# Linear attention into two expert layers: batches 2 and 3 of k and v loaded in the first visits, x written over its squares, eight weight preparations ahead of the units, stores one step behind

## The chip, the cores and the metric

The kernel runs on one core of a Trainium2 chip. The metric is the device time of one execution in microseconds (us). A core has TensorE (PE, matrix products), VectorE (DVE), ScalarE (ACT), GpSimd (POOL) and SyncE (SP); here SP issues every DMA, in program order. Each engine runs its own instructions in order and waits on semaphores of the others. TensorE's clock has two levels, 1.2 and 2.4 GHz; a granted clock of 1.00 is the upper one.

## The reference

```
kv  = einsum('bhsd,bhse->bhde', k, v)            # 4 batches, 8 heads, 576 tokens, 64 wide
out = einsum('bhsd,bhde->bhse', q, kv)
out = out / sqrt(mean(out*out, -1) + 1e-6) * g_norm
x   = out as [2304 tokens, 512]
h   = x @ w_in                                   # 512 -> 2048
x   = (h * sigmoid(h)) @ w_out                   # 2048 -> 512
out = ((x @ w_a) * (x @ w_b)) @ w_out2           # 512 -> 1536 -> 512
```

q, k, v and g_norm are float32. The weight matrices come as float64 values; the kernel reads them as pairs of 32-bit words, rebuilds a float32 number from them, and splits that into a high and a low part, so that a product of two float32 matrices is three passes of TensorE (high by high, low by high, high by low).

## The kernel before, in words

The 2304 tokens are six blocks of 384 (a block is called j). Work goes in steps. A step belongs to one slice of 128 of the 2048 hidden columns and one block: `h_mm` (12 matmuls into `hp`), the gate `g` on ACT (L409), its high part `gh` on ACT (L355) and low part `gl` on DVE (L360), and 12 matmuls `x1p` (L371) that add the slice of the step before to the four output columns. `VISITS` lists which block takes which slices, and a running number g counts the steps: g = 4 to 31 are the first visits (blocks 0, 1 and 2), where the raw weights `raw_wi` and `raw_wo` also arrive and are decoded on DVE (shift L302, low word L308, sign L315, low part L330); g = 32 to 63 are the visits of blocks 2 and 3, where the weights are already there. After that come eight units u, each a seven-product (Winograd) scheme for two slices and the blocks 4 and 5 together (`seven`, `unit`; matmuls X_h, Y_h, V_h, Z_h; DVE additions L660, L663, L792). Then phase 3 computes products with w_a, w_b and w_out2 by the same scheme.

What else has to happen is hung on the steps by number: `at(g, f)` runs f after the x1p of step g, and `early[g]` runs it between `gh` and `gl` of step g, so that DVE does it ahead of the `gl` for which the next x1p waits. `at_unit(h, f)` hangs f on hook h of the units, four hooks to a unit. Hung there are:

- attention: `load_kv` and `load_kvt` (L114, L122) bring k and v, `kv_pair` multiplies them (`kvps`, L180) and copies the result to `kvc`; `load_q_blocks`, `turn_q` (DVE transpose `qT`, L153), `attend` (matmuls `ao` L214, squares `sq` on ACT L220, sum `ss` on DVE L225, the power -0.5 `rr` on POOL L230), `norm_mul` (`xn`, DVE L235) and the transposes `xtp` (PE L248). Before, k and v of batches 2 and 3 are loaded at g = 33 to 51 and multiplied two steps later;
- `sums(u)` (L728 to L739): sums of the decoded w_in slices that the units need, stored to DRAM (`hsd`) and read back;
- `prepare(wa or wb, pair)`: loads, decodes and combines two slices of w_a or w_b and stores the result (`wd`) for phase 3. There are twelve. Before, six start at g = 36, 42, 48, 54, 58 and 62 and six in the units;
- `combine(0, kt)`: the sums of blocks 0 and 1 of the second layer's input (`hB`, `hT`, `T`), stored to `xcd`.

Buffers are pools that rotate: `page` 37 tiles of 4 KB, `mid` 6 tiles (qT, xn, T and hT and others, in order of allocation), and two tiles of squares that carry the 1e-6 in an extra column. A new tile waits for the last reader of the one whose place it takes. SP issues DMAs in order, so a DMA that waits for a buffer holds up all behind it.

Of the kernel before, what the change touches and what calls it, by code (L numbers as in the profile page):

```python
# [59 lines left out]
def tile_linattn_moe_moe2(ctx: ExitStack, tc: tile.TileContext, q, k, v, g_norm,  # L60
# [21 lines left out]
    sq = [sb.tile([P, CH, 2, D + 1], F32, tag=f"sq{i}", name=f"sq{i}") for i in range(2)]  # L82
# [13 lines left out]
    def mid(shape, dt, name):  # L96
        return sb.tile(shape, dt, tag="mid", bufs=6, name=name)

    def six(shape, dt, name):
# [6 lines left out]
           for b in range(2) for p in range(NP)}  # L106
    kvc.update({(b, p): kvc[b % 2, p] for b in range(2, B) for p in range(NP)})
# [110 lines left out]
    def norm_square(j, p):  # L218
        sq.reverse()
        nc.scalar.activation(sq[0][:, :, :, 0:D], ao[j, p], AF.Square, scale=D ** -0.5)  # L220
        xn[j, p] = sq[0]

    def norm_mean(j, p):
        ss = sb.tile([P, CH, 2], F32, tag="ss", bufs=3, name=f"ss_{j}_{p}")
        nc.vector.reduce_sum(ss, xn.pop((j, p)), axis=AX.X)  # L225
        rms[j, p] = ss
# [6 lines left out]
    def norm_mul(j, p):  # L233
        xn[j, p] = mid([P, CH, 2, D], F32, f"xn_{j}_{p}")
# [196 lines left out]

    def combine(d, kt, place, blocks=None, keep=None, home=None):
# [47 lines left out]
    def prepare(kind, p):  # L480
# [24 lines left out]
        def rest():  # L505
            for f in wait.pop(0):
                f()
# [171 lines left out]
    PLACES = {"mid": 6, "sig": 2, "gh": 2, "gl": 2}  # L679
    ab = {}  # L680

    def products(d, p, after=None, more=(), more_b=()):

        a = {}
        for n, got in enumerate(seven_ab(d, p, 0, "mid")):
            if n == 2 and after is not None:
                after()
            if got is not None:
                f, i, z, u = got
                t = a[f, i] = sb.tile([P, TB], F32, tag="mid", bufs=6, name=f"a_{d}_{p}_{f}{i}")  # L690
# [29 lines left out]
    def sums(u):  # L720
# [5 lines left out]
        def add():  # L726
            for t, (hi, lo) in zip(s, (w0, w1_)):
                nc.vector.tensor_add(t[:, 0].bitcast(F32), hi.bitcast(F32), lo.bitcast(F32))  # L728
            a11, a12, a21, a22 = (t[:, 0, h * H2:(h + 1) * H2].bitcast(F32) for t in s for h in range(2))
# [6 lines left out]
        def split():  # L736
            for t in s:
                nc.scalar.copy(t[:, 0], t[:, 1].bitcast(F32))
                nc.vector.tensor_sub(t[:, 1], t[:, 1].bitcast(F32), t[:, 0].bitcast(F32))  # L739
# [7 lines left out]
        return add, split, store  # L747
# [142 lines left out]
    at(base[5] - 2, load_kvt, 2)  # L890
    at(base[5] + 6, load_kvt, 3)
    for i, (p, j) in enumerate([(p, 3) for p in range(NP)] + [(p, j) for p in (0, 2, 1, 3) for j in (4, 5)]):
        g0 = base[5] + 1 + 2 * i
        if j != 5:
            b = 2 if j == 3 else 3
            at(g0 - 2, load_kv, b, p)
            at(g0, kv_pair, b, p)
# [10 lines left out]

    for n in range(2 * NPAIR):
        load, steps = prepare(("wa", "wb")[n % 2], n // 2)  # L910
        if n < 6:
            g0 = base[5] + (4, 10, 16, 22, 26, 30)[n]
# [9 lines left out]
        else:  # L922
            h0 = 1 + 5 * (n - 6)
            if n == 6:
                at(base[6] + 15, load)
            else:
                at_unit(h0 - 3, load)
# [330 lines left out]
```

## Time and profile before

| | us |
|---|---|
| median of 3 runs | 881.21 (881.09 to 881.83) |
| profiled execution | 884.84 |
| its span, first to last instruction | 883.0 |
| PE busy | 861.4 (98%) |
| DVE busy | 604.3 (68%) |
| ACT busy | 330.7 (37%) |
| POOL busy | 51.9 (6%) |

The profiled execution is 3.6 us above the median of the runs. Its mean granted TensorE clock is 0.995. A row of the chain of waits has its start, its duration and what ran; a row of a timeline has start, duration, engine, line, operation, tiles and, in brackets, how long the engine sat idle before it and what it waited for. A row of the view by stretches has the stretch, then busy time and count of each engine in it, the granted clock, the share of the DMA engines and GB/s. A row of waits has who waited for whom, us in total, times, and the longest. A busy PE is a modelled figure: a matmul's end is put some way past the start of the next one.

### The profile page before, as it was taken

To read this page: it belongs to the slowest core of one execution; us is meant where nothing else is said; L and a number is where in the kernel's file an instruction comes from. 1 tells how busy PE (TensorE), PEld (TensorE's weight loads), DVE (VectorE), ACT (ScalarE), POOL (GpSimd) and SP (SyncE) were. 2 spreads that over 40 slices of the span, in tenths; PEclk is the share of its full clock that TensorE was granted. 3 is DMA by queue.
4 is the path that set the end of the run, shared out by engine and by line. 5 is a ranking of instruction groups with operands and counts; after the bars stand their busy time and mean duration, and the time that the engine had idled before them with its cause. 6 is when DMAs were issued, how large, how long until landed. Compare 5 with 4: busy or idle time off the path is not lost.

```text
span 883.0 us, 13575 instructions
## 1 busy us (share of the span) xinstructions
PE 861.4 (98%) x5015; PEld 818.0 (93%) x5015; DVE 604.3 (68%) x1153; ACT 330.7 (37%) x670; POOL 51.9 (6%) x53
## 2 busy tenths in 40 slices
PE   7999999999899999999999999999999999999998
PEld 4799999999899999999999999999999999999996
DVE  3879997848356778787626788886556665545555
ACT  4666654426334555545323523321232211121110
POOL 4420001001111100000000000000000000000000
PEclk9999999999899999999999999999999999999999
DMA  9942890866675378999499789496787476765001
GB/s 268 354 178 98 227 331 15 287 209 193 195 235 178 107 265 313 377 372 355 185 422 419 309 335 339 172 368 263 252 292 266 155 248 265 283 217 191 1 1 71
DMA packets 123650, 212.19 MB, mean 240 GB/s; under 512 B 41024, under 2 KB 85568, under 8 KB 123584
## 3 DMA queue, kind: packets, MB, share of 16 engines
q1 hardware_dynamic: 123584, 211.33, 67.8%
q8 instruction: 39, 0.64, 0.3%
q14 instruction: 27, 0.22, 0.1%
HBM read 143.92 MB, written 67.37 MB: 239 GB/s over the span
## 4 chain that ended last, share of the span: by engine, by line
PE 84%; DVE 7%; DMA 4%; SPq 2%; issue 2%; ACT 1%; POOL 0%; DVEq 0%; POOLq 0%; ACTq 0%
PE x1p L371 19%; PE op L830 17%; PE hp L345 12%; PE Z_a L653 4%; PE V_b L653 4%; PE X_b L653 4%; PE Z_b L653 4%; PE X_a L653 4%; PE V_a L653 4%; PE Y_b L653 2%; PE Y_a L653 2%; PE Z_h L653 2%; DMA kvt<-in_v_dram 2%; PE V_h L653 2%; PE X_h L653 1%
## 5 line engine op out<-in xcount | busy, mean ns | idle before, releaser
L371 PE MATMUL x1p<-gh,wo 128*128 128x384 f32 x768 | 193.9, 335 | 0.0
L371 PEld LDWEIGHTS x1p<-gh,wo 128*128 128x128 f32 x768 | 138.9, 188 | 0.0
L371 PE MATMUL x1p<-gl,wo 128*128 128x384 f32 x384 | 127.9, 337 | 1.4 <-DVE gl L360 1.4
L345 PE MATMUL hp<-xh,wi 128*128 128x384 f32 x512 | 104.8, 345 | 0.4 <-ACT xh L252 0.3
L360 DVE TENSOR_TENSOR gl<-g,gh 128x384 fp32r<-128x384 f32 x96 | 54.2, 565 | 59.0 <-ACT gh L355 58.6
L345 PEld LDWEIGHTS hp<-xh,wi 128*128 128x128 f32 x512 | 89.3, 190 | 1.8 <-ACT xh L252 1.0
L830 PE MATMUL op<-wp,ab 128*128 128x512 f32 x360 | 83.4, 390 | 0.0
L712 ACT CAST ab<-a 128x384 fp32r<-128x384 f32 x72 | 37.0, 514 | 115.3 <-DVE a L706 58.2
L830 PEld LDWEIGHTS op<-wp,ab 128*128 128x128 f32 x360 | 67.4, 188 | 13.7
L371 PEld LDWEIGHTS x1p<-gl,wo 128*128 128x128 f32 x384 | 72.0, 188 | 2.5 <-DVE gl L360 2.3
L838 DVE TENSOR_TENSOR o<-op,o 128x512 f32<-128x512 f32 x90 | 60.4, 685 | 16.4 <-PE op L830 16.3
L830 PE MATMUL op<-w,ab 128*128 128x512 f32 x288 | 66.9, 390 | 0.0
L830 PEld LDWEIGHTS op<-w,ab 128*128 128x128 f32 x288 | 53.9, 188 | 10.9
L355 ACT CAST gh<-g 128x384 fp32r<-128x384 f32 x96 | 49.3, 514 | 28.4 <-PE x1p L371 26.2
L345 PE MATMUL hp<-xl,wi 128*128 128x384 f32 x256 | 55.7, 338 | 0.0
L409 ACT ACTIVATE g<-hp 128x384 f32<-128x384 f32 x64 | 31.3, 490 | 63.8 <-PE hp L345 63.7
L230 POOL TENSOR_TENSOR rr<-ss,nhalf 128x6 f32<-128x6 f32 x24 | 35.7, 1491 | 228.0 <-DVE ss L225 227.9
L345 PEld LDWEIGHTS hp<-xl,wi 128*128 128x128 f32 x256 | 45.9, 190 | 0.4 <-DVE xl L256 0.3
L653 PE MATMUL X_a<-xc,wp 128*128 128x384 f32 x216 | 43.7, 337 | 0.7 <-ACT u_a L658 0.7
L653 PE MATMUL Z_a<-xc,wp 128*128 128x384 f32 x216 | 43.4, 335 | 0.1
L653 PE MATMUL Z_b<-xc,wp 128*128 128x384 f32 x216 | 43.4, 335 | 0.1
L653 PE MATMUL V_b<-xc,wp 128*128 128x384 f32 x216 | 43.3, 335 | 0.0
(177 smaller groups left out, 1424.1 us busy)
## 6 DMA issues: line engine op xcount, KB each, us to landing
wp<-wd SPq DMA_DIRECT2D x114, 512.0 KB, 6.4
xc<-xcd SPq DMA_DIRECT2D x21, 768.0 KB, 8.5
hw<-hsd SPq DMA_DIRECT2D x24, 512.0 KB, 7.3
raw_wi<-in_moe_w_in_dram SPq DMA_DIRECT2D x16, 512.0 KB, 7.5
raw_wo<-in_moe_w_out_dram SPq DMA_DIRECT2D x16, 512.0 KB, 7.5
hsd<-hs SPq DMA_DIRECT2D x16, 512.0 KB, 4.2
raw_wa<-in_moe_w_a_dram SPq DMA_DIRECT2D x12, 512.0 KB, 6.6
wd<-s_wa SPq DMA_DIRECT2D x12, 512.0 KB, 3.6
```

The costliest lines, as they stand in the source:

```text
L230: nc.gpsimd.tensor_tensor(r, rms[j, p], nhalf, op=ALU.pow)
L345: nc.tensor.matmul(o, w[wp][:, kt * P:(kt + 1) * P], x[key][:, kt, :], start=(n == 0), stop=(n == 3 * KD - 1))
L355: nc.scalar.copy(gh, src)
L360: nc.vector.tensor_sub(gl, src, gh.bitcast(F32))
L371: nc.tensor.matmul(acc[vi][c], w[wp][:, c * P:(c + 1) * P], gg[vi, s][g], start=(s == s0 and i == 0), stop=(s == s1 - 1 and i == 2))
L409: nc.scalar.activation(g, o, AF.Silu)
L653: nc.tensor.matmul(b[bank], w(name, wq, kt), x(i, xq, kt), start=(fresh and k == 0), stop=(k == 5), skip_group_check=True)
L712: nc.scalar.copy(o[:, 0], t)
L830: nc.tensor.matmul(o, ab[d, p, f, n][:, g, ts], wp[p, 7 + f][:, wq * DM:(wq + 1) * DM], start=(k == 0), stop=(k == 5))
L838: nc.vector.tensor_add(t, o, t)
```

## The change

k and v of batches 2 and 3 are loaded and multiplied at g = 11 to 26. Batch 3's products get tiles of their own (`kvc`), batch 2 still takes those of batch 0. For blocks 3 to 5 `xn` is written over the tile that held its squares, and POOL writes the 1e-6 column again before each of these squares; `mid` goes from 6 tiles to 5. Eight preparations of w_a and w_b start at g = 34, 38, ... 62 and four in the units, at other hooks. The stores of `prepare` go through a list that `flush` empties one step later. The parts of `sums` are spread over more hooks and begin at other steps. `combine(0)` is hung before the preparations, so that it comes first where both share a step.

```diff
@@ -79,7 +79,9 @@
-    sq = [sb.tile([P, CH, 2, D + 1], F32, tag=f"sq{i}", name=f"sq{i}") for i in range(2)]
+    sqs = [sb.tile([P, TB + 2 * CH], F32, tag=f"sq{i}", name=f"sq{i}") for i in range(2)]
+    sq = [(t.rearrange("p (c r d) -> p c r d", c=CH, r=2),
+           t[:, 0:TB].rearrange("p (c r d) -> p c r d", c=CH, r=2)) for t in sqs]
     x1d = dr.tile([NB - 2, P, KD, TB], F32, tag="x1d", name="x1d")
@@ -94,7 +96,7 @@
     def mid(shape, dt, name):
-        return sb.tile(shape, dt, tag="mid", bufs=6, name=name)
+        return sb.tile(shape, dt, tag="mid", bufs=5, name=name)
@@ -103,8 +105,8 @@
     kvc = {(b, p): sb.tile([P, P], F32, tag=f"kvc{b}_{p}", name=f"kvc_{b}_{p}")
-           for b in range(2) for p in range(NP)}
-    kvc.update({(b, p): kvc[b % 2, p] for b in range(2, B) for p in range(NP)})
+           for b in (0, 1, 3) for p in range(NP)}
+    kvc.update({(2, p): kvc[0, p] for p in range(NP)})
     qs, qT, xn, ao, rms, xt = {}, {}, {}, {}, {}, {}
@@ -217,12 +219,14 @@
         sq.reverse()
-        nc.scalar.activation(sq[0][:, :, :, 0:D], ao[j, p], AF.Square, scale=D ** -0.5)
+        if j >= 3:
+            nc.gpsimd.memset(sq[0][0][:, :, :, D:], 1e-6)
+        nc.scalar.activation(sq[0][0][:, :, :, 0:D], ao[j, p], AF.Square, scale=D ** -0.5)
         xn[j, p] = sq[0]
...
         ss = sb.tile([P, CH, 2], F32, tag="ss", bufs=3, name=f"ss_{j}_{p}")
-        nc.vector.reduce_sum(ss, xn.pop((j, p)), axis=AX.X)
+        nc.vector.reduce_sum(ss, xn[j, p][0], axis=AX.X)
         rms[j, p] = ss
@@ -231,7 +235,7 @@
     def norm_mul(j, p):
-        xn[j, p] = mid([P, CH, 2, D], F32, f"xn_{j}_{p}")
+        xn[j, p] = xn[j, p][1] if j >= 3 else mid([P, CH, 2, D], F32, f"xn_{j}_{p}")
         nc.vector.tensor_mul(xn[j, p], ao.pop((j, p)), rms.pop((j, p)).unsqueeze(3).broadcast_to([P, CH, 2, D]))
@@ -429,6 +433,14 @@
+    fresh_, due = [], []
+
+    def flush():
+        while due:
+            due.pop(0)()
+        due.extend(fresh_)
+        fresh_.clear()
+
@@ -503,8 +515,9 @@
         def rest():
-            for f in wait.pop(0):
-                f()
+            sub, *put_ = wait.pop(0)
+            sub()
+            fresh_.extend(put_)
@@ -676,7 +689,7 @@
-    PLACES = {"mid": 6, "sig": 2, "gh": 2, "gl": 2}
+    PLACES = {"mid": 5, "sig": 2, "gh": 2, "gl": 2}
     ab = {}
@@ -687,7 +700,7 @@
                 f, i, z, u = got
-                t = a[f, i] = sb.tile([P, TB], F32, tag="mid", bufs=6, name=f"a_{d}_{p}_{f}{i}")
+                t = a[f, i] = sb.tile([P, TB], F32, tag="mid", bufs=5, name=f"a_{d}_{p}_{f}{i}")
                 if u is None:
@@ -723,9 +736,11 @@
-        def add():
+        def whole():
             for t, (hi, lo) in zip(s, (w0, w1_)):
...
+
+        def add():
             a11, a12, a21, a22 = (t[:, 0, h * H2:(h + 1) * H2].bitcast(F32) for t in s for h in range(2))
@@ -733,9 +748,12 @@
-        def split():
+        def high():
             for t in s:
...
+
+        def low():
+            for t in s:
                 nc.vector.tensor_sub(t[:, 1], t[:, 1].bitcast(F32), t[:, 0].bitcast(F32))
@@ -744,7 +762,7 @@
-        return add, split, store
+        return whole, add, high, low, store
@@ -887,14 +905,13 @@
-    at(base[5] - 2, load_kvt, 2)
-    at(base[5] + 6, load_kvt, 3)
+    for b, g0 in ((2, 11), (3, 18)):
+        at(g0, load_kvt, b)
+        for p in range(NP):
+            at(g0 + 2 * p - p // 3, load_kv, b, p)
+            at(g0 + 3 + 2 * p - p // 3, kv_pair, b, p)
     for i, (p, j) in enumerate([(p, 3) for p in range(NP)] + [(p, j) for p in (0, 2, 1, 3) for j in (4, 5)]):
         g0 = base[5] + 1 + 2 * i
-        if j != 5:
-            b = 2 if j == 3 else 3
-            at(g0 - 2, load_kv, b, p)
-            at(g0, kv_pair, b, p)
         at(g0 - 5, load_q_blocks, j, p)
@@ -906,10 +923,17 @@
+    todo = [f for kt in range(2) for f in combine(0, kt, mid)]
+    for n, fs in enumerate(todo):
+        for f in fs:
+            if n % 2:
+                at(base[5] + 1 + n // 2, f)
+            else:
+                early.setdefault(base[5] + 1 + n // 2, []).append(f)
     for n in range(2 * NPAIR):
         load, steps = prepare(("wa", "wb")[n % 2], n // 2)
-        if n < 6:
-            g0 = base[5] + (4, 10, 16, 22, 26, 30)[n]
+        if n < 8:
+            g0 = base[5] + 2 + 4 * n
             at(g0 - 3, load)
@@ -920,20 +944,13 @@
         else:
-            h0 = 1 + 5 * (n - 6)
-            if n == 6:
+            h0 = 3 + 7 * (n - 8)
+            if n == 8:
                 at(base[6] + 15, load)
             else:
-                at_unit(h0 - 3, load)
+                at_unit(h0 - 4, load)
             for i, f in enumerate(steps):
                 at_unit(h0 + i, f)
-    todo = [f for kt in range(2) for f in combine(0, kt, mid)]
-    for n, fs in enumerate(todo):
-        for f in fs:
-            if n % 2:
-                at(base[5] + 1 + n // 2, f)
-            else:
-                early.setdefault(base[5] + 1 + n // 2, []).append(f)
     made = []
@@ -942,10 +959,12 @@
     for u in range(NF1 // 2):
-        g0 = (8, 12, 15, 18, 25, 26, 28, 29)[u]
+        g0 = (7, 10, 14, 17, 23, 25, 27, 29)[u]
         at(g0, begin_sums, u)
-        at(g0 + 1, lambda u: made[u][1](), u)
-        at(g0 + 2, lambda u: made[u][2](), u)
+        early.setdefault(g0 + 1, []).append(lambda u=u: made[u][1]())
+        at(g0 + 1, lambda u: made[u][2](), u)
+        early.setdefault(g0 + 2, []).append(lambda u=u: made[u][3]())
+        at(g0 + 3, lambda u: made[u][4](), u)
     homes = []
@@ -1057,9 +1076,9 @@
     nc.gpsimd.memset(nhalf, -0.5)
-    for t in sq:
+    for t, _ in sq:
         nc.gpsimd.memset(t[:, :, :, D:], 1e-6)
-    for t in [kvc[b, p] for b in range(2) for p in range(NP)]:
+    for t in [kvc[b, p] for b in (0, 1, 3) for p in range(NP)]:
         nc.gpsimd.memset(t, 0.0)
@@ -1158,8 +1177,8 @@
                     then += [d1.begin, d1.step]
-                between = [d1.begin] if j < 2 else early.get(g, [])
-                step1(vi, s, prev, side.get(-g, []) + then + side.get(g, []), between)
+                between = ([d1.begin] if j < 2 else []) + early.get(g, [])
+                step1(vi, s, prev, [flush] + side.get(-g, []) + then + side.get(g, []), between)
                 prev = (vi, s)
@@ -1171,10 +1190,10 @@
             left = []
-            for h, k in enumerate((0, 2, 3, 6)):
+            for h, k in enumerate((0, 2, 4, 6)):
                 hooks[k] += inner.get(4 * u + h, [])
-            hooks[3] += both(g)
-            hooks[6] += both(g + 1)
+            hooks[3] += [flush] + both(g)
+            hooks[6] += [flush] + both(g + 1)
             for n, to, i in (((0, 1, 0), (0, 1, 2)) if u == 0 else ()) + (
@@ -1182,7 +1201,7 @@
             g += 2
-        for f in left:
+        for f in left + [flush, flush]:
             f()
...
             gg[8, s] = split_pair(g1[s // 4][:, s % 4], f"5_{s}")
```

Three places show how the order of the work moves. The first is SP's queue. Before, the loads of batch 3's first pair (`kv_3_0`, k and v of heads 0 and 1) stand behind stores of `combine` and `prepare` (`xcd`, `wd`), in step 39, two steps ahead of the product that needs them:

```order
L122 DMA kvt_3_2448<-in_k_dram 64x8x64
L122 DMA kvt_3_2448<-in_v_dram 64x8x64
L145 DMA qb_5_0_2467<-in_q_dram 32x12x32 x4
L430 DMA wd_72<-s_0_wa0_2425 128x1024
L430 DMA wd_72<-s_1_wa0_2426 128x1024
L430 DMA wd_72<-m_wa1_2333 128x512
L114 DMA kv_3_0_2533<-in_k_dram 128x2x256
L114 DMA kv_3_0_2533<-in_v_dram 128x2x256
L282 DMA raw_wb0_2536<-in_moe2_w_b_dram 128x4x256
```

After, SP issues them in step 18, between the raw loads of the slices 13 to 15 (`raw_wi`, `raw_wo`) and the stores of `sums`:

```order
L286 DMA raw_wo13_1428<-in_moe_w_out_dram 128x1024
L147 DMA qb_2_3_1456<-in_q_dram 32x12x32 x4
L124 DMA kvt_3_1474<-in_k_dram 64x8x64
L124 DMA kvt_3_1474<-in_v_dram 64x8x64
L116 DMA kv_3_0_1478<-in_k_dram 128x2x256
L116 DMA kv_3_0_1478<-in_v_dram 128x2x256
L286 DMA raw_wi14_1500<-in_moe_w_in_dram 128x4x256
L286 DMA raw_wo14_1558<-in_moe_w_out_dram 128x1024
L116 DMA kv_3_1_1595<-in_k_dram 128x2x256
L116 DMA kv_3_1_1595<-in_v_dram 128x2x256
L760 DMA hsd_69<-wi_6_866 128x1024
L761 DMA hcd_70<-wi_7_960 128x2x256
```

In the queue the k load of `kv_3_0` goes from row 133 to row 83 counted from the start; the raw loads of slices 14 and 15 now stand behind loads that were not there.

The second place is ACT's queue near step 44, where `combine(0, 1)` makes its last piece, `hT4_0_1`. Before:

```order
L409 ACTIVATE g_5_11_2737<-hp_5_11_2724 128x384
L355 CAST gh_5_11_2739<-g_5_11_2737 128x384
L428 CAST hB21_0_1_2744<-x1_0_704 128x384
L428 CAST a_wb0_2770<-m_wb0_2718 128x512
L428 CAST hT4_0_1_2775<-T4_0_1_2722 128x384
L409 ACTIVATE g_5_12_2793<-hp_5_12_2780 128x384
L355 CAST gh_5_12_2795<-g_5_12_2793 128x384
L888 ACTIVATE xf_4_2822<-xtp_4_0_2825,g2_64 128x384
L220 ACTIVATE sq0_66<-ao_5_0_2830 128x6x64
```

After:

```order
L413 ACTIVATE g_5_11_2827<-hp_5_11_2814 128x384
L359 CAST gh_5_11_2829<-g_5_11_2827 128x384
L432 CAST hB21_0_1_2831<-x1_0_712 128x384
L432 CAST hT4_0_1_2856<-T4_0_1_2808 128x384
L432 CAST a_wa1_2861<-m_wa2_2810 128x512
L413 ACTIVATE g_5_12_2883<-hp_5_12_2870 128x384
L359 CAST gh_5_12_2885<-g_5_12_2883 128x384
L906 ACTIVATE xf_4_2911<-xtp_4_0_2914,g2_64 128x384
L224 ACTIVATE sq0_66<-ao_5_0_2919 128x6x64
```

The rows read alike, but with five `mid` tiles instead of six `hT4_0_1` takes the place of `qT_5_0`, so this cast now waits for the matmuls `ao_5_0` on PE, and the gate of slice 12 stands behind it.

The third place is DVE's queue at the first unit. Before, from the additions `u2_h_0` and `u3_h_0` to the first `gl` of the units:

```order
L660 TENSOR_TENSOR u2_h_0_3835<-Y_h_0_3849,u2_h_0_3835 128x384
L663 TENSOR_TENSOR u3_h_0_3864<-V_h_0_3857,u2_h_0_3835 128x384
L403 COPY x1_3_3866<-x1p_6_1_3088 128x384
L403 COPY x1_3_3866<-x1p_6_3_3090 128x384
L429 TENSOR_TENSOR s_0_wb2_3839<-s_0_wb2_3839 128x512
L429 TENSOR_TENSOR s_1_wb2_3840<-s_1_wb2_3840 128x512
L429 TENSOR_TENSOR m_wb5_3774<-m_wb5_3774 128x256
L302 TENSOR_SCALAR m_wa6_3887<-m_wa6_3887 128x512
L308 SCALAR_TENSOR_TENSOR m_wa6_3887<-raw_wa6_3823,m_wa6_3887 128x512
L315 SCALAR_TENSOR_TENSOR m_wa6_3887<-raw_wa6_3823,m_wa6_3887 128x512
L792 TENSOR_TENSOR h_0_11_3919<-Z_h_0_3912,u3_h_0_3864 128x384
L360 TENSOR_TENSOR gl_4_0_3921<-g_4_0_3897,gh_4_0_3899 128x384
```

After:

```order
L673 TENSOR_TENSOR u2_h_0_3909<-Y_h_0_3922,u2_h_0_3909 128x384
L676 TENSOR_TENSOR u3_h_0_3937<-V_h_0_3930,u2_h_0_3909 128x384
L407 COPY x1_3_3939<-x1p_6_1_3181 128x384
L407 COPY x1_3_3939<-x1p_6_3_3183 128x384
L810 TENSOR_TENSOR h_0_11_3979<-Z_h_0_3972,u3_h_0_3937 128x384
L364 TENSOR_TENSOR gl_4_0_3981<-g_4_0_3966,gh_4_0_3968 128x384
L433 TENSOR_TENSOR s_0_wb3_3912<-s_0_wb3_3912 128x512
L433 TENSOR_TENSOR s_1_wb3_3913<-s_1_wb3_3913 128x512
L433 TENSOR_TENSOR m_wb7_3848<-m_wb7_3848 128x256
L810 TENSOR_TENSOR h_0_10_3996<-V_h_0_3930,u2_h_0_3909 128x384
```

Three splits (L429) and three decode operations of `m_wa6` no longer stand ahead of `h_0_11`; the splits of the preparation before come behind `gl`, and `m_wa6` is decoded earlier.

## Rows read from the trace of the kernel before

**Rows 1.** busy time by stretch, core 0: the first visits, one dip, the units
```profile
67.00:130.00 63.00, 62.64 (x363) 62.33 (x362) 59.05 (x116) 38.96 (x75) 1.84 (x1) 1.00 0.73 218
...
200.00:240.00 40.00, 36.31 (x245) 34.32 (x244) 23.93 (x49) 17.02 (x39) 5.41 (x4) 0.91 0.62 195
...
340.00:430.00 90.00, 87.52 (x501) 86.75 (x501) 70.79 (x143) 47.56 (x95) 0.00 (x0) 1.00 0.88 330
```

**Rows 2.** waits of PE over the whole span
```profile
PE kvps L180 <- DMA kv<-in_v_dram: 4.8, 3, 2.6
...
PE ao L214 <- DVE qT L153: 2.6, 3, 1.1
...
PE Z_h L653 <- DVE h L792: 1.4, 1, 1.4
...
PE V_h L653 <- DVE h L792: 1.0, 1, 1.0
...
PE x1p L371 <- DVE gl L360: 1.4, 3, 0.8
```

**Rows 3.** chain of waits from 205 to 250 us
```profile
220.95 5.60 DMA kv<-in_v_dram
...
226.64 1.33 PE kvps L180 x20
...
227.98 4.14 PE hp L345 x12
...
232.12 2.52 PE x1p L371 x12
...
236.98 2.11 PE hp L345 x12
```

**Rows 4.** timeline of PE, one kv pair on the upper clock
```profile
181.65 0.69 PE L180 MATMUL kvps<-kv 128*64 128x64 f32 x16
182.17 0.29 PE L180 MATMUL kvps<-kvt 128*64 128x64 f32 x4
```

**Rows 5.** timeline of PE, the wait at 131 us
```profile
132.30 0.91 PE L214 MATMUL ao<-kvc,qT 128*128 128x128 f32 x6 [1.08 <-DVE qT L153]
```

**Rows 6.** timeline of DVE, 125 to 130 us
```profile
125.53 0.68 DVE L330 TENSOR_TENSOR wi<-m_wi,wi 128x512 fp32r<-128x512 f32 x1
...
126.13 0.68 DVE L315 SCALAR_TENSOR_TENSOR m_wo<-raw_wo,m_wo 128x512 uint32<-128x512 uint32 x1
...
127.53 0.55 DVE L360 TENSOR_TENSOR gl<-g,gh 128x384 fp32r<-128x384 f32 x1
...
129.30 0.56 DVE L235 TENSOR_TENSOR xn<-ao,rr 128x384 f32<-128x384 f32 x1 [1.22 <-POOL rr L230]
```

**Rows 7.** timeline of POOL, two powers
```profile
127.43 1.84 POOL L230 TENSOR_TENSOR rr<-ss,nhalf 128x6 f32<-128x6 f32 x1 [77.65 <-DVE ss L225]
...
143.56 1.32 POOL L230 TENSOR_TENSOR rr<-ss,nhalf 128x6 f32<-128x6 f32 x1 [6.84 <-DVE ss L225]
```

**Rows 8.** timeline of DVE at 197 us
```profile
197.10 0.58 DVE L153 STREAM_TRANSPOSE qT<-qb 128x384 f32<-128x384 f32 x1 [4.22 <-PE xtp L248]
```

**Rows 9.** waits of SP from 44 to 450 us
```profile
SPq L745 <- DVE hs L739: 74.3, 5, 34.1
```

**Rows 10.** DMA issues of raw_wo: KB each, us from issue to landing
```profile
raw_wo<-in_moe_w_out_dram SPq DMA_DIRECT2D x16, 512.0 KB, 7.5
```

**Rows 11.** tile kv, its loads
```profile
DMA to landing us min/median/max: 2.6/4.3/8.8
```

**Rows 12.** groups of DVE, 67 to 200 us, a 256-wide sum
```profile
L731 DVE TENSOR_TENSOR hs<-hs 128x256 f32<-128x256 f32 x8 | 3.4, 426 | 0.3
```

**Rows 13.** costliest groups of the page, the high part on ACT
```profile
L355 ACT CAST gh<-g 128x384 fp32r<-128x384 f32 x96 | 49.3, 514 | 28.4 <-PE x1p L371 26.2
```

**Rows 14.** waits of ACT from 60 to 340 us
```profile
ACT hT L428 <- PE ao L214: 14.9, 2, 8.8
```

**Rows 15.** timeline of POOL at the start
```profile
1.45 1.08 POOL L1063 MEMSET kvc<- 128x128 f32 x7
```

## The prediction

> **What bounds the kernel now.** I read the busy shares by stretch first. PE is the bound: 87.5 of 90 us in the units, 62.64 of 63 us in the first visits [rows 1]. So only time in which PE waits, or runs on the lower clock, can be won. The one stretch with a lower clock is 200 to 240 us, at 0.91, with PE busy for 36.3 of 40 us [rows 1]. The waits of PE then name who ended them: the loads of k and v 4.8 us in three waits, the longest 2.6; the turned q 2.6 us in three; `gl` 1.4 us in three; DVE's additions `h` in the units 1.4 and 1.0 us [rows 2]. Last I followed the chain through 205 to 250 us for the worst one: a v load that took 5.60 us to land, then `kvps`, then 12 matmuls of `hp` in 4.14 us and 12 of `x1p` in 2.52, where a later row has 2.11 for the same 12 of `hp` [rows 3]. A wait row understates its loss by about 0.17 us, since a 128x384 matmul is shown with 0.34 us and the next starts 0.17 us after it; I add that to each.
>
> **What can be won at most.** Five places. (a) At 226 us: 2.64 + 0.17 for the wait. Behind it the clock is at the lower level: `hp` takes 4.14 - 2.11 = 2.03 too long, `x1p` 2.52 - 2.11 = 0.41, and the pair itself 1.33 against 182.17 + 0.29 - 181.65 = 0.81 for one at the upper level, so 0.52 [rows 3, 4]. Together 5.8. (b) The three waits for `qT`: 2.6 + 0.5 = 3.1 [rows 2], of which the one at 131 us is 1.08 + 0.17 = 1.25 [rows 5]. (c) The three for `gl`: 1.4 + 0.5 = 1.9. (d) The two for `h`: 2.4 + 0.3 = 2.7. Sum 13.5. The other two kv waits are at the start, which the change does not touch.
>
> **The change part by part.**
>
> *k and v in the first visits.* The wait of (a) goes, with its clock: at g = 33 to 53 no load is waited for any more, because `kv_3_0` is multiplied in step 21. Worth 5.8. Each of the eight pairs still costs PE its 0.81 us, now between g = 14 and 26; that is moved and not added. What is late next is the raw weights. kv loads land in 2.6 to 8.8 us [rows 11], raw loads in 7.5 [rows 10], and SP issues in order: `raw_wo14` takes the page of a k or v tile that PE reads in step 19 and cannot be issued earlier, about 121 us on the clock of before. It then lands at 121 + 7.5 = 128.5, and its decode stands on DVE and ACT for about 129.7. So some 1 us is left, and `raw_wi14`, two steps before, has about none. Bounds: nothing, or a wait as long as the present one with the clock lost, 5.8. I take nothing, since DMA is busy 0.73 there [rows 1] and the stores of `sums`, on which SP stood 74.3 us waiting for DVE in five waits, one of 34.1 [rows 9], now enter SP's queue a step later, when their data is done.
>
> The Trainium skill's "DMA: Bandwidth & Descriptors", section "Anatomy of one DMA", gives a fit of about 2.0 us plus bytes over 436 GB/s, for loads issued by GpSimd; for these 512 KB an estimate from it is 3.2 us. The trace has 7.5, more than twice that, and I go by the trace; by the fit the raw loads would have 4 us to spare, the first and second rival below would have no ground, and the sum would not change.
>
> *POOL.* Four more `kvc` memsets at the start: seven take 1.08 us [rows 15], so some 0.6 us, ahead of the memset of `kvt` that the first products read. If nothing hid it, that is +0.6; PE waits there for k and v loads anyway [rows 2], so I take 0. The twelve memsets of the squares' extra column are smaller still and run on an engine with 5.4 us of work in 40 [rows 1]: 0 to 0.15 us each if one ended a wait; 0. Each waits for the transposes of the `xn` two attends back, done by then; behind it on POOL stands only the power of its own attend, and ACT's square waits for it.
>
> *Batch 2's `kvc` and DVE at g = 20 to 22.* At 131 us `qT` came late because DVE stood 1.22 us for the power `rr` [rows 6]. In the changed order a kv pair's 0.81 us lies on PE ahead of this `ao`, so DVE is given that much. Between 0 and 1.25 remain; I take 1.25 - 0.81 = 0.4 left, 0.85 won.
>
> This power took 1.84 us; one that ran with DVE idle took 1.32 [rows 7]. Beside the first DVE ran `gl`, a subtraction of two SBUF tiles [rows 6]. The Trainium skill's "SBUF — State Buffer", section "Who interferes with whom", says that a DVE instruction with two SBUF inputs and a GpSimd one that reads SBUF block each other; the trace agrees, with 0.52 us. It speaks against this change, because `sums` and `prepare` are made of such instructions and now stand beside more of the powers: by it the 0.85 would be 0.3.
>
> *`xn` over its squares, `mid` from 6 to 5.* Before, `qT` took the place of an older `xn`, so it waited 4.22 us for PE's transposes and then came late [rows 8]; there are two such places, at 197 and 235 us, each 0.76 + 0.17 = 0.93. After, no `xn` of these blocks is in `mid`, and the places are freed by stores or casts. Both go: 1.9. The new wait is `hT4_0_1` on ACT in step 44, for `ao_5_0` on PE. Behind it on ACT stand a cast of `a_wa1`, the gate of slice 12 and its `gh`; on DVE two subtractions, four 256-wide sums of 0.43 [rows 12], and the `gl`. From the end of `ao_5_0` that is two ACT casts of 0.51 [rows 13] or so, then on DVE 0.60 for a 512-wide operation (they start 0.60 apart [rows 6]), four of 0.35 to 0.43 and 0.56: about 3.8 us. PE has one `hp` of 2.11 and two matmuls, 2.45, before it needs that `gl`. So PE waits 1.4. From below the cost is nothing, if the kernel's ACT waits for `ao` of before, 14.9 us in two [rows 14], are a measure: they ended no wait of PE. I take 1.4, because here the gate stands right behind. It comes where before a `gl` wait of 0.75 + 0.17 was.
>
> *Sums and preparations on other steps.* At g = 8 to 11 the rows of DVE between two `gl`, counted from the order at 0.60 for 512-wide, 0.47 for 384-wide and 0.35 for 256-wide, come to 5.6, 4.0, 5.2 and 5.6: 20.4 us against four steps of 4.2, so 3.6 too much. `gl` can lead by one `hp` and two matmuls, 2.45. PE waits about 1.2, where before 0.36 + 0.17 stood in step 10. At 211 us the prepare rows ahead of `gl` move to other steps, and 0.46 goes. In (c) then: 0.53 + 0.46 + 0.92 = 1.9 before, 1.2 + 1.4 = 2.6 after, so 0.7 lost. Ahead of the units DVE gets 14.3 us more over g = 34 to 63: two preparations, less the sums that move up. In 200 to 240 it is busy 23.9 of 40 [rows 1], and the heaviest step there has 6.2 against 4.2 with light ones beside it, so it holds.
>
> *Units.* Four preparations instead of six. Ahead of `h_0_11` three splits (0.60 + 0.60 + 0.35) and three decode operations (0.35 + 0.60 + 0.60), 3.1 us, go, against a wait of 1.4; at 367 us four sums and a split leave in the same way. I take 2.5 of the 2.7.
>
> **The sum.** 5.8 + 0.85 + 1.9 - 0.7 + 2.5 = 10.3. From the profiled execution, 884.84 - 10.3 = 874.5; it stands 3.6 above the median of 881.21, so the runs should have 870.9. Phase 3 is left as it is: PE is full there, and of `mid` its tiles wait a product longer back.
>
> **Rivals.** 1. Half of it is given back in 75 to 140 us. DVE is busy 59 of 63 us there [rows 1], the raw loads have 0 to 1 us of room, and `sums` come a step earlier. Two waits of the size of the present kv one, 2.8 each without a lost clock: 10.3 - 5.6 = 4.7, time 876.5. Against it: DVE's total in the stretch is the same.
> 2. Slower. The same raw loads, but late by more than a few us: SP stands at `raw_wo14` for its page and everything behind it is late too, `raw_wi15` and `raw_wo15` among it. From the point where PE waits as long as 2.6 us the clock is lost as in [rows 3], and each costs 5.8. Three of them, 17.4, against 10.3 won: 888.3. Against it: such pages were waited for before, and PE lost no clock there (1.00 in 67 to 130 [rows 1]).
> 3. No change: what PE gets back is waited for at the next `gl`, because DVE with 14.3 us more is the bound from g = 32 on. Then (a) to (d) turn into `gl` waits, 880.5. Against it: DVE busy about 24 + 69 of 140 us there and 14.3 more make 77%.
> 4. All of it, with no new wait: 13.5, 867.7.
>
> **How the numbers follow.** Forecast 0.56 (7.5 to 12.5 won, 868.7 to 873.7); rival 1 0.20 (3 to 7.5, 873.7 to 878.2); rival 2 0.10; rival 3 0.07; rival 4 0.07. The range goes from 867.5 to 879.5, which leaves out rival 2 and most of rival 3. No change means within 0.2%, 1.8 us, about what this kernel's measurement tells: 0.07. Slower by more is rival 2, 0.10; faster 0.83.
>
> **What would show it.** In the changed profile 200 to 240 us has clock 1.00 and no wait of PE for k or v after the start; the waits for `qT` fall to one below 0.6 us; the waits for `h` are gone or under 0.3; two new `gl` waits stand near 85 us (1.2) and near step 44 (1.4, behind ACT's `hT`). I am wrong if ACT's first decode operation waits for a raw load between 110 and 140 us and PE for `hp` or `gl` behind it, or if the units still show a wait for `h` of over 1 us.

## The result and the profile after

| | before | after |
|---|---|---|
| median, us | 881.52 (881.09 to 883.85, 4 runs) | 872.15 (871.73 to 873.01, 4 runs) |
| profiled execution, us | 884.84 | 872.3 |
| its span, us | 883.0 | 870.5 |
| PE busy, us | 861.4 (98%) | 858.1 (99%) |
| DVE busy, us | 604.3 (68%) | 605.6 (70%) |

The ratio is 0.989, interval 0.9871 to 0.9909: 9.4 us faster, where 10.3 were forecast (870.9). A second comparison, on the chip of most of the experiments, gave 871.23 against 880.37, ratio 0.9891 (0.9869 to 0.9913). Line numbers of the changed kernel are higher: L375 is x1p, L364 `gl`, L349 `hp`, L216 `ao`, L252 `xtp`, L182 `kvps`, L434 a store of `wd` or `xcd`, L763 one of `hsd`.

Stretches of the changed kernel, with the columns of [rows 1]:

```profile
67.00:130.00 63.00, 62.49 (x422) 60.90 (x420) 59.33 (x117) 38.04 (x77) 1.45 (x2) 1.00 0.84 253
...
200.00:240.00 40.00, 40.00 (x249) 39.53 (x248) 33.46 (x68) 20.85 (x43) 6.50 (x8) 1.00 0.85 281
...
340.00:430.00 90.00, 90.00 (x520) 90.00 (x519) 56.91 (x112) 39.66 (x80) 0.00 (x0) 1.00 0.75 279
```

The dip at 200 to 240 us is gone: 40.00 of 40 us at clock 1.00, where [rows 1] have 36.31 at 0.91. In the units PE is full, and DVE has 56.9 us of work there and not 70.8.

All waits of PE that answer to [rows 2], and the largest others:

```profile
PE x1p L375 <- DVE gl L364: 1.6, 2, 1.1
PE ao L216 <- ACT kvc L188: 1.5, 2, 1.2
PE kvps L182 <- DMA kvt<-in_v_dram: 1.2, 2, 0.6
...
PE kvps L182 <- DMA kv<-in_v_dram: 0.2, 1, 0.2
```

No wait for `qT` or `h` is left, and the 1.2 and 0.2 us for loads stand in the first 60 us. From 60 to 450 us the view has one row, the two waits for `gl`. These are the two that the prediction named:

```profile
86.47 0.44 PE L375 MATMUL x1p<-gl,wo 128*128 128x384 f32 x1 [0.51 <-DVE gl L364]
```

```profile
243.01 0.45 PE L375 MATMUL x1p<-gl,wo 128*128 128x384 f32 x1 [1.11 <-DVE gl L364]
```

The first is the one that the prediction put down to DVE's surplus over steps 8 to 11, the second stands at step 44. ACT's timeline there, columns as in [rows 6]:

```profile
239.26 0.52 ACT L432 CAST hT<-T 128x384 fp32r<-128x384 f32 x1 [5.79 <-PE ao L216]
239.68 0.62 ACT L432 CAST a_wa<-m_wa 128x512 fp32r<-128x512 f32 x1
240.20 0.48 ACT L413 ACTIVATE g<-hp 128x384 f32<-128x384 f32 x1
240.72 0.51 ACT L359 CAST gh<-g 128x384 fp32r<-128x384 f32 x1
```

ACT sat idle for 5.79 us until the matmuls `ao` had run, with the cast of T4 at the head of its queue and the gate and `gh` behind it. The chain goes from there through DVE to the matmul:

```profile
238.56 0.68 PE ao L216 x6
...
239.26 0.52 ACT hT L432
239.78 0.53 ACT a_wa L432
...
242.41 0.56 DVE gl L364
...
243.01 2.02 PE x1p L375 x10
```

From the end of `ao` at 239.24 to the end of `gl` at 242.97 are 3.7 us; 3.8 were forecast.

Where the time came from is read at two places that both traces have: the first `hp` after 60 us and the first X_a of phase 3. Between them lie 401.8 us before and 389.8 after, 12.0 less. Ahead of them the two spans differ by 0.6, behind them by nothing. Another profile of the kernel before (below) has 400.1 between them, so the same stretch is 10.3 less against that one.

### The profile page after: what moved, and what is told of

It is laid out like the page before. It is cut to its first block, busy times and chain, and to the rows that moved or that the text cites. A ratio compares the mean times of both kernels' runs of the same rounds, so it can differ in the third digit from the quotient of the medians.

```text
span 870.5 us, 13610 instructions
## 1 busy us (share of the span) xinstructions
PE 858.1 (99%) x5014; PEld 815.8 (94%) x5015; DVE 605.6 (70%) x1153; ACT 330.8 (38%) x670; POOL 54.7 (6%) x69
## 4 chain that ended last, share of the span: by engine, by line
PE 89%; DVE 6%; issue 1%; ACT 1%; POOL 0%; DVEq 0%; ACTq 0%
PE x1p L375 21%; PE op L848 16%; PE hp L349 14%; PE Z_a L666 4%; PE X_b L666 4%; PE V_b L666 4%; PE X_a L666 4%; PE Z_b L666 4%; PE V_a L666 4%; PE Y_b L666 2%; PE X_h L666 2%; PE Z_h L666 2%; PE V_h L666 2%; PE Y_a L666 2%; PE ao L216 2%
## 5 line engine op out<-in xcount | busy, mean ns | idle before, releaser
L375 PE MATMUL x1p<-gh,wo 128*128 128x384 f32 x768 | 193.8, 335 | 0.0
L375 PEld LDWEIGHTS x1p<-gh,wo 128*128 128x128 f32 x768 | 138.4, 188 | 0.3 <-ACT gh L359 0.3
L375 PE MATMUL x1p<-gl,wo 128*128 128x384 f32 x384 | 127.6, 336 | 1.6 <-DVE gl L364 1.6
L349 PE MATMUL hp<-xh,wi 128*128 128x384 f32 x512 | 103.3, 342 | 0.4 <-ACT xh L256 0.3
L364 DVE TENSOR_TENSOR gl<-g,gh 128x384 fp32r<-128x384 f32 x96 | 54.2, 566 | 52.3 <-ACT gh L359 52.0
L349 PEld LDWEIGHTS hp<-xh,wi 128*128 128x128 f32 x512 | 88.2, 188 | 1.8 <-ACT xh L256 1.0
L375 PEld LDWEIGHTS x1p<-gl,wo 128*128 128x128 f32 x384 | 71.9, 188 | 2.3 <-DVE gl L364 2.3
L349 PE MATMUL hp<-xl,wi 128*128 128x384 f32 x256 | 55.2, 335 | 0.0
L349 PEld LDWEIGHTS hp<-xl,wi 128*128 128x128 f32 x256 | 45.2, 188 | 0.5 <-DVE xl L260 0.5
```

Of the source, the lines that this page charges most:

```text
L349: nc.tensor.matmul(o, w[wp][:, kt * P:(kt + 1) * P], x[key][:, kt, :], start=(n == 0), stop=(n == 3 * KD - 1))
L364: nc.vector.tensor_sub(gl, src, gh.bitcast(F32))
L375: nc.tensor.matmul(acc[vi][c], w[wp][:, c * P:(c + 1) * P], gg[vi, s][g], start=(s == s0 and i == 0), stop=(s == s1 - 1 and i == 2))
```

## The experiments

Each was timed against the kernel before on the same chip, which had medians of 880.2 to 881.1 there. "Stretch" is the time between the two places just named, in the profile of that kernel. Profiles differ at their start, too: the step whose `hp` comes first after 60 us above, the 57th ahead of the units, began between 61.5 and 63.5 us in them, in one at 65.7, so the stretch says more than the span.

**The kernel before again.**

> The kernel before, unchanged, for the granted clock and the span of each run. The prediction took 5.8 us at the wait for batch 3's v load, of which 3.0 are the lower clock behind it. First theory: the clock falls in ordinary runs too; then each run shows a mean granted clock near 0.995 and the profile a stretch of 0.91 at 200 to 240 us. Rival: the profiled execution was an unusual one, since it stood 3.6 us above the median; then ordinary runs show a clock of 1.000, and a new profile has the wait but no lower clock, with a span near 879.5.

880.89 (878.65 to 883.26, 12 runs). With the 23 runs of before beside them there are 35: in 16 the granted clock is 0.998 or less, and they took 880.7 to 883.3 us; in 19 it is 0.999 or 1.000, and they took 878.7 to 881.0. So the clock falls in some runs only, and where it does not, the kernel is about 2 us faster: neither theory holds for every run. The mean clock of a run does not say where it fell; in two profiles further down (the stores at once, the later cast) it fell in the first 40 us only. The profiled run of this kernel is one in which it fell, to 0.96 over 200 to 240 us. The chain at the load, to be held against [rows 3]:

```profile
220.86 5.06 DMA kv<-in_v_dram
...
226.01 0.94 PE kvps L180 x20
226.96 3.68 PE hp L345 x12
230.63 2.08 PE x1p L371 x12
```

The load took 5.06 and not 5.60, PE waited 2.0 and not 2.6, and behind it `hp` took 3.68 and `x1p` 2.08, so there was less of the lower clock. The place costs about 2.2 + 1.6 + 0.1 = 3.9 here and 5.8 in the first profile. Where the clock holds it should be the wait alone; no profile of such a run is there to show it.

**One load a step earlier, in the kernel before.**

```diff
-            at(g0 - 2, load_kv, b, p)
+            at(g0 - 3 if i == 4 else g0 - 2, load_kv, b, p)
```

> The kernel before with one load moved: k and v of batch 3's first pair one step earlier, ahead of three stores of prepared weights at which SP stands. First theory: this load is late because SP stands at those stores; the wait of 2.2 to 2.8 us at 224 us goes, and with it the lower clock behind it: by the two profiles of before so far 3.8 to 5.8 us, so 874.5 to 876.6. Rival: DVE's work is late there as well, and the waits for the turned q and gl at 211 to 250 us grow by what PE gets back: less than 1.5 us faster.

881.29 (879.95 to 883.17), ratio 1.0015 (1.0005 to 1.0024): not faster at all, stretch 399.2. The wait for the load is gone from its place, and PE waits 2.28 us a step later:

```profile
PE xtp L248 <- DVE xn L235: 2.8, 2, 2.3
```

```profile
224.21 5.50 DMA xcd<-hB
...
229.83 0.57 DVE xn L235
230.45 0.56 PE xtp L248 x3
```

The chain reads upwards from PE: the transposes `xtp` waited for `xn`, `xn` on DVE waited for its place in the pool `mid`, and that place was free only when a store of `hB`, issued at 224.21, had landed 5.50 us later. The same wait stands in the trace of the kernel before, where PE came to the transposes only at 234.6 us, behind the load and the lower clock, so that it ended no wait of PE:

```profile
229.94 0.56 DVE L235 TENSOR_TENSOR xn<-ao,rr 128x384 f32<-128x384 f32 x1 [6.35 <-DMA xcd<-hB]
```

The place at 224 us had two causes, and the first hid the second. In all 11 runs the mean clock is 0.998 or less; of the 14 runs of before beside them, in one. The rival is nearer, with another wait than it named.

**x over its squares alone, in the kernel before.** The edits of `sq`, `norm_square`, `norm_mean` and `norm_mul` as in the change, the pool left at six:

```diff
-        xn[j, p] = mid([P, CH, 2, D], F32, f"xn_{j}_{p}")
+        xn[j, p] = xn[j, p][1] if j >= 3 else mid([P, CH, 2, D], F32, f"xn_{j}_{p}")
```

> The kernel before with x of blocks 3 to 5 written over its squares, and nothing else (the pool keeps six tiles). First theory: the two waits for the turned q at 197 and 235 us go, 0.93 each: 1.9 faster, 879.4 to 879.8. Rival: the q turned at 235 us is late for another reason, or its time is taken up by the next wait for gl: 0 to 1 us faster.

878.13 (876.73 to 879.42), ratio 0.9978 (0.9969 to 0.9988): 2.2 faster, as the first theory has it. But the profile shows more than two waits gone:

```profile
PE x1p L375 <- DVE gl L364: 3.1, 4, 1.7
...
PE ao L216 <- DVE qT L155: 1.1, 1, 1.1
```

The waits at 197 and 235 us are gone, and so is the one for the kv load, without that load being moved; a wait for `gl` of 1.7 us has come at 215 us. The stretch is 396.3 in this profile, 3.8 and 5.5 less than in the two of before. Counted from the first `hp`, SP issued that v load 1.0 us earlier than in the first profile of before, and it took 4.57 us and not 5.60; so x in `mid` was part of what made the load late. But PE also came to the product 0.9 us later, behind the wait for `gl`: part of the wait was passed on and not won. The terms of the sum are not independent.

**k and v early alone, in the kernel before.**

```diff
-    at(base[5] - 2, load_kvt, 2)
-    at(base[5] + 6, load_kvt, 3)
+    for b, g0 in ((2, 11), (3, 24)):
+        at(g0, load_kvt, b)
+        for p in range(NP):
+            at(g0 + 2 * p - p // 3, load_kv, b, p)
+            at(g0 + 3 + 2 * p - p // 3, kv_pair, b, p)
...
-            at(g0 - 2, load_kv, b, p)
-            at(g0, kv_pair, b, p)
```

> The kernel before with one part of the change alone: k and v of batch 2 loaded from step 11 and of batch 3 from step 24, so that no tile of its own is needed. First theory (the load and its clock cost 5.8 in every run): 875.4 to 876.2. Rival (the wait alone, 2.8, and the clock falls only in some runs): 878.2 to 879.0. Third theory (the gain is given back at the waits for gl and for the turned q that follow): above 880.5. In its profile no wait of PE for k or v after the start; the waits at 197, 235 and in the units stay.

888.56 (888.19 to 888.94), ratio 1.0097 (1.0084 to 1.011): 8 us slower, which none of the three theories has. The chain between 164 and 187 us:

```profile
164.56 4.70 DMA hsd<-hs
...
169.36 0.70 DVE hs L728
...
172.10 0.54 DVE xl L256
...
172.69 1.36 PE kvps L180 x20
...
178.79 4.50 DMA hsd<-hs
...
183.38 0.70 DVE hs L728
```

The kv tiles take pages. DVE's next sum (L728) then finds no free page until a store of an earlier sum has landed. The 4.70 and 4.50 are the landings of two such stores; DVE itself stands longer, and in the kernel before it has no such wait:

```profile
DVE hs L728 <- DMA hsd<-hs: 9.0, 4, 6.0
```

Everything on DVE behind it is late, `xl` and `gl` among it, and PE waits 4.4 and 3.8 us; the clock is 0.85 over 160 to 190 us. SP is part of the circle: it stands 9.0 us at a load of k, until `kvps` at 172.69 has read the page, and the second of the stores is issued behind that load. The change has the loads earlier still for batch 3 and spreads the sums.

**The sums at the steps of before, in the changed kernel.**

```diff
-        g0 = (7, 10, 14, 17, 23, 25, 27, 29)[u]
+        g0 = (8, 12, 15, 18, 25, 26, 28, 29)[u]
```

> The changed kernel with the sums of the second layer begun at the steps of before (8, 12, 15, 18, 25, 26, 28, 29). First theory: in the run with k and v alone DVE stood 4.7 and 4.5 us for stores of these sums, because pages were short and the sums came in a row at 25 to 29; with k and v early and the old steps this comes back, 4 to 10 us slower than the changed kernel. Rival: that was the place of batch 3's products in that run; here they are at 21 to 26, and the result is within 1 us of the changed kernel.

886.92 (886.63 to 888.35), ratio 1.008 (1.0067 to 1.0093): some 16 us slower than the changed kernel with its 0.9891. The size is beyond what was expected, and so is the place. DVE stands for no store of the sums. SP stands 27.3 us at a load of w_a (L286), for a page that a decode of w_a still reads:

```profile
SPq L286 <- DVE m_wa L319: 27.3, 1, 27.3
```

```profile
195.11 0.39 SPq L286
...
209.63 2.14 DMA xcd<-hT
...
212.53 1.62 PE ao L216 x6
```

What is queued behind it on SP comes out one by one from 195 to 209 us, the store of `hT` that the turned q needs among the last; DVE stands 10.0 us for it, and PE 6.9 for that q, with a clock of 0.79 over 200 to 240 us. The first theory is right in that the queue stands for a page; but it is SP that stands, and what frees the page is no store of a sum. How the old steps of the sums bring this about is not shown.

**The stores of `prepare` at once, in the changed kernel.**

```diff
-            fresh_.extend(put_)
+            for f in put_:
+                f()
```

> The changed kernel with the stores of the prepared weights issued at once, not one step later. First theory (of the prediction, that the delay only keeps SP from standing at data that is not done): SP's loads behind the stores come later by up to the wait of a store, and PE sees little of it: 0 to 1.5 us slower than the changed kernel. Rival: the delay holds pages longer and costs something; then it is faster. With four preparations in the units no wait of DVE for a store is expected in either.

877.77 (875.24 to 880.38), ratio 0.9966 (0.9951 to 0.9982), against 871.23 of the changed kernel on that chip: 6.5 slower. Not all of that is shown to be the price of the stores. In this profile the clock is low early on, long before the first store of `prepare`:

```profile
30.00:40.00 10.00, 9.67 (x61) 8.47 (x62) 8.19 (x13) 5.29 (x13) 5.75 (x5) 0.66 1.06 387
```

This is the profile in which the stretch begins at 65.7 us; it is 394.0 against 389.8, so 4.2 us are lost behind that point, where the clock is 1.00 from 60 to 450 us. In 8 of the 12 runs the mean clock is 0.998 or less, in none of the six of the changed kernel; the other four took 875.2 to 877.3, on average 4.5 more than the changed kernel. So the stores cost 4 to 4.5 us, three times the most that was allowed for; whether the lower clock of the other runs has to do with them is open. The waits of SP between 200 and 430 us, and two of PE:

```profile
SPq L434 <- DVE s_wb L541: 22.6, 3, 11.3
SPq L434 <- DVE a_wb L433: 22.4, 2, 11.2
...
SPq L434 <- DVE a_wa L433: 13.1, 2, 7.9
```

```profile
PE V_h L667 <- DMA hw<-hcd: 1.7, 1, 1.7
PE ao L216 <- DVE qT L155: 1.4, 1, 1.4
```

SP stands 58 us in all at these three kinds of stores, whose data DVE has still to make; in the changed kernel the same view has 22.0 us for `a_wb`, 5.9 for `a_wa` and none for `s_wb` of that line. Behind it the loads are late: PE waits 1.4 us for the turned q and 1.7 for a weight of the units; with the longer matmuls right behind them these two places make the 4.2.

**Six preparations ahead and six in the units, in the changed kernel.** 

```diff
-        if n < 8:
-            g0 = base[5] + 2 + 4 * n
+        if n < 6:
+            g0 = base[5] + (4, 10, 16, 22, 26, 30)[n]
...
-            h0 = 3 + 7 * (n - 8)
+            h0 = 1 + 5 * (n - 6)
...
-            for h, k in enumerate((0, 2, 4, 6)):
+            for h, k in enumerate((0, 2, 3, 6)):
```

> The changed kernel with the preparations of w_a and w_b where they were before: six ahead of the units, six within them. First theory: the two waits for h in the units come back, 2.5 us, and the preparations that now fall together with the sums of the second layer cost nothing more: 874.4 to 875.2. Rival: the units were helped by the later stores and not by the count; then 872.0 to 873.0. In the profile of the first theory PE waits for h of about 1.4 and 1.0 us stand in the first three units.

898.01 (896.29 to 898.58), ratio 1.0201 (1.0187 to 1.0214): some 27 us slower than the changed kernel. In the units:

```profile
PE V_h L666 <- DVE u_h L676: 8.7, 3, 4.9
PE Z_h L666 <- DVE h L810: 7.2, 3, 5.4
```

```profile
DVE s_wa L541 <- DMA wd<-s_wb: 6.7, 3, 5.8
DVE s_wa L540 <- DMA wd<-a_wb: 5.0, 1, 5.0
```

DVE's sums of the weights stand for pages that delayed stores still hold, up to 5.8 us, and the additions `h` and `u_h` behind them are late; the clock is 0.91 over 340 to 430 us. The next run took the delay away as well, with the edit of the stores above.

> The changed kernel with six preparations ahead of the units and six within, as before, and their stores at once, as before. First theory: the 26 us that six and six cost with the delayed stores come from the delay, since in the units a preparation's pages are then held half a unit longer and DVE stood for the store; at once, only the waits for h of before and the cost of stores at once are left: 877 to 882. Rival: the count of six in the units on the changed hooks is what costs; then above 890.

873.12 (872.65 to 874.05), ratio 0.9923 (0.9908 to 0.9937), better than the first theory said. Of the 27 us the delay makes 24 (2.8%). What is left in the profile from 60 to 430 us:

```profile
PE Z_h L667 <- DVE h L811: 1.4, 1, 1.4
PE x1p L375 <- DVE gl L364: 0.5, 1, 0.5
PE V_h L667 <- DMA hw<-hcd: 0.4, 1, 0.4
```

These are the waits for `h` and a weight, 1.4 and 0.4 us, and no other but the one at step 11; the stretch is 390.6 against 389.8. So eight and four in place of six and six, each with the stores that suit it, is worth 1 to 3 us. It wins 2.4 us in the units and gives 1.7 back ahead of them, where this run has no wait at step 44 (the first `X_h` of the units comes at 325.2 us here and at 327.2 in the changed kernel, with starts 0.4 apart). Stores at once cost at most the 0.4 for the weight with this order of preparations and 4 to 4.5 us with the other; a step later they cost 24 with this one. The delay belongs to the eight and four.

**x back in the pool of five, in the changed kernel.**

```diff
-        xn[j, p] = xn[j, p][1] if j >= 3 else mid([P, CH, 2, D], F32, f"xn_{j}_{p}")
+        xn[j, p] = mid([P, CH, 2, D], F32, f"xn_{j}_{p}")
```

> The changed kernel with x back in the pool mid, which keeps its five tiles (POOL still writes the extra column). First theory (the prediction's terms add up): the two waits of 0.9 us for the turned q come back, 1.9 slower than the changed kernel. Second theory, from the runs with one load moved and with x alone: a tile of mid that x holds stands for a store to land, as where PE waited 2.3 us for x behind a store of 5.5 us, and SP's order spreads it: 4 us or more slower than the changed kernel, 875 or above, with waits of PE for x or the turned q of over 2 us at 190 to 250 us.

874.2 (872.99 to 874.66), ratio 0.9926 (0.991 to 0.9942), against 0.9891 of the changed kernel on another chip: 0.35%, 3 us, with both intervals wide enough for 1 to 5. The stretch is 391.3, 1.5 more than that of the changed kernel. By the runs it falls between the two theories, by the profile it is near the first in size, though not by the two waits that the first named. From 60 to 450 us PE waits for one turned q, and longer at step 44:

```profile
PE x1p L375 <- DVE gl L364: 2.1, 2, 1.6
PE ao L216 <- DVE qT L155: 0.7, 1, 0.7
```

**Two repairs of the changed kernel.** With the last cast of T4 a step and a half later:

```diff
+    todo[21:] = [todo[21][1:], (), todo[21][:1], todo[22]]
```

> The changed kernel with the last cast of the second layer's sums (hT4_0_1) moved behind the matmuls ao_5_0, for which it waits, by one and a half steps. First theory: the wait for gl of 1.1 us at 243 us comes from this cast, with the gate of slice 12 queued behind it; it goes, and the kernel is 1.0 to 1.3 us faster than the changed one. Rival: DVE's four sums and the a_wa subtraction ahead of that gl are late anyhow; then 0 to 0.4 faster and the wait stays.

870.6 (869.9 to 871.66) against 871.23 (870.82 to 872.73) for the changed kernel on the same chip.

> The changed kernel again, on the chip that runs the three below, as their measure. 872 to 873, 8 to 10 us below the kernel before.

The wait at step 44 is gone and the stretch 388.2, 1.6 shorter; of that the medians show 0.6, and the runs of the two kernels overlap. The cast was the cause of the wait, as the prediction had it. With the second group of sums begun at step 11 besides:

```diff
-        g0 = (7, 10, 14, 17, 23, 25, 27, 29)[u]
+        g0 = (7, 11, 14, 17, 23, 25, 27, 29)[u]
```

> As the run before, and the second group of sums one step later (begun at step 11 and not 10). First theory: the 0.5 us wait for gl at 86 us is DVE's surplus over steps 8 to 11 and goes; in all 1.5 to 2.0 us faster than the changed kernel, near 870.4. Rival: the surplus moves to steps 12 and 13 and the wait with it; then no faster than the run before.

869.28 (868.97 to 869.57), ratio 0.9869 (0.9847 to 0.9891), 2.0 below the changed kernel and faster than both. The stretch is 387.4, and from 60 to 450 us PE waits for nothing that the view lists:

```profile
200.00:340.00 140.00, 140.00 (x842) 138.43 (x841) 110.17 (x222) 78.20 (x161) 17.80 (x21) 1.00 0.73 246
```

The kernel before with the early k and v and the new sums together, for which 875 to 878 was expected, gave no time: in that order the program waits for itself (a deadlock). So it stays open what the new sums alone do for the early loads. k and v at their old steps with the rest of the change were not tried; since x alone took the wait for the load away, that is the gap that matters most.

## Why the prediction was right, and where it was not

*The dip at 226 us.* It went, worth 5.8 in the profile that the sum was made against. In a second profile the same place cost 3.9, and in more than half of the runs the clock held, which is most of why the medians moved by 9.4 and the profiles by 12.5. So this term was too big for an ordinary run: taking 3.6 us off the profiled time for the median does not take the lower clock out of the 5.8. The step's reason was too short: it said that the wait goes because the product is made in step 21. With the load alone moved, the kernel gained nothing, because x in `mid` stood for a store at the same place; with x alone moved, the wait for the load went too. How much of the dip each of the two parts takes away in the changed kernel is not shown.

*The turned q.* Both waits at 197 and 235 us went, 0.93 each, as forecast. That x alone brought 2.2 us is no proof of these 1.9, since the wait for the load went there too and one for `gl` came. The 0.4 us that were to stay at 131 us did not: 0.85 was forecast, 1.25 came.

*`gl`.* The surplus of 1.2 us at step 11 is 0.51 + 0.17 = 0.7; moving one group of sums by a step took it away. The 1.4 at step 44 is 1.11 + 0.17 = 1.3, with the cast, the queue behind it and the chain as told; taking the cast away took the wait away. Together 2.0 in place of 2.6, so 0.1 was lost and not 0.7.

*The units.* The waits for `h` went, 2.7 in place of 2.5. Six and six with their stores at once brought one of them back, 1.4 us, and a wait of 0.4 for a weight.

*The sum.* The places give 5.8 + 1.25 + 1.9 - 0.1 + 2.7 = 11.6 in the profile, where the stretch got 12.0 shorter: the forecast had 1.3 too little outside the dip. For a run whose clock holds, the dip is 2.8 by the wait, and the places give 8.6; on the chip of the second comparison such runs of before have a median of 879.6, 8.3 above the changed kernel. So the mechanism is right in the main, but that 10.3 came so near to the 9.4 of the medians is in part luck: too much at the dip and too little elsewhere.

*The stores.* This is the step that failed. The prediction has no term for the stores of `prepare`, which puts them at nothing. Stores at once cost 4 to 4.5 us in the changed kernel. The wait is not PE's but SP's, and it shows in no row of PE before; with eight preparations ahead it would have come into being. The sum did not suffer, since the delay is part of the change, but the 10.3 was right for a kernel in which this price had not to be paid, and the text gave no reason for that. What it did say of stores, that those of `sums` find their data done a step later, did not come true either: SP stood 74.3 us at them before [rows 9] and still stands 58.0 after. The raw loads were in time all the same.

```profile
SPq L763 <- DVE hs L757: 58.0, 12, 28.2
```

*Rivals.* Raw loads were not late: PE has 62.49 of 63 us in 67 to 130 us, and the wait there is the 0.51 of step 11. Rival 2's mechanism, a page for which SP or DVE stands and a queue behind it, with the clock lost, is what three of the experiments ran into, at 8 to 27 us; in the changed kernel itself no such wait reaches PE. Rival 3 was wrong: from step 34 to the units DVE is busy 107.3 us and not 96.7, some 11 more where 14.3 were counted, and PE has 40.00 of 40 us in 200 to 240 us.

## What to carry to other kernels

When one engine issues all transfers in order and the buffers rotate, price a moved load or store by what it holds (its page) and by what stands behind it in the queue, not by the wait it removes; parts of such a change can each lose what together they win, so test them by taking one out as well as by putting one in. A long wait in a trace may have a second cause behind the one that is named: look at what else was released last at that place. And make sums against more than one profile, where runs of one kernel differ by 3 us; before a difference is put down to an edit, count off the same step in both profiles and look at the clock ahead of it.

## What was not expected of the hardware

A wait of PE of 2.0 us was followed in the second profile of before by the lower clock (`hp` 3.68 us in place of 2.1), one of 1.7 us for `gl` in the run with x alone was not (`hp` 2.11). The runs of the kernel before spread over 2.0 to 6.0 us on one chip (877.9 to 883.91 at the widest), those of the changed kernel over 1.9 and of the last version over 0.6.

In the changed kernel a power on POOL that ran beside two subtractions for the sums and a `gl` on DVE took 2.77 us (at 148.9 us), one beside two such subtractions 1.32 (at 157.6); both kinds of DVE instruction read two inputs in SBUF. So the rule that the prediction cites from the Trainium skill's "SBUF — State Buffer", section "Who interferes with whom", is borne out by the first and not by the second, and PE waited for neither. Nor does the pair from which the prediction took its 0.52 us come out the same again: the power beside one `gl` that took 1.84 us before took 1.37 after (at 129.5 us), and the gain that was to shrink to 0.3 by that rule was 1.25.
